# v cast to bfloat16 inside its own transfer, issued by GpSimd, in an attention and token-mixing kernel

## The chip, the cores and the metric

The kernel runs on one core of a Trainium2 chip. A core has a matrix engine (PE in the profile; its weight loads are listed apart as PEld), a vector engine (DVE), a scalar engine (ACT), GpSimd (POOL) and a sync engine (SP), which here issues transfers and computes nothing. Each engine works through its own instructions in order and waits on semaphores of the others. Transfers run on 16 DMA engines, whoever issues them. The metric is the device time of one execution in microseconds; the kernel before took 190.26, 190.16 and 189.40 us in three runs, a median of 190.16 us.

## The reference

Two stages in sequence, for 8 batches, 12 heads, 448 positions and a head size of 64, all in float32 outside:

```
scores = q @ k^T / sqrt(64) - log(448)          # per batch and head
attn   = 1 / (1 + exp(-scores))                 # a sigmoid, no softmax
x      = attn @ v, heads laid side by side      # (8, 448, 768)
wq, wk = x @ w_q, x @ w_k                       # (8, 448, 64)
W_tok  = wq @ wk^T / sqrt(64)
out    = relu(W_tok @ x) @ w_out                # (8, 448, 768)
```

## The kernel before

**Tiling.** The 96 heads are taken four at a time: 24 quads (8 batches of 3 quads). For one quad, q, k and v are 448 KB of float32 each; a tile has 128 partitions with 2 x 448 elements in each, because 64 partitions hold 7 positions apiece of a head, and two pairs of heads lie in the two halves. A quad has seven blocks of positions. For a block `scores` (L303) makes four 64-row matmuls into a pair of PSUM banks, ACT turns them into a bfloat16 tile with one sigmoid (L308), and `values` (L321) multiplies v into it, summing over the seven blocks. After the seventh the sum is copied to the x tile (L330, L328). The token-mixing stage of a batch (L361 and L344 transposes, L387 and L400 projections, L431, L471 and L483 mixing, L516, L556 and L600 the last product) is woven between the attention work of later quads.

**How the inputs come in.** SP issues the loads in float32 into six buffers `lds`, used in rotation by everything that is loaded: q, k and v of each quad and the weights. `pump_loads` issues the next entry of the list `ORDER` when the entry six places earlier has been cast (`ring[-6] not in cast`). From there the data are cast to bfloat16. GpSimd (engine "g") does most casts, at L198 (v, and q and k of some quads), L188 (q and k of the other quads, in another layout, followed for most of them by three pairs of copies at L157, L160 and L163) and L737 and L741 (weights); entries of `ORDER` with a dot are cast by DVE. q and k have two bfloat16 buffers each, or two for both where they share one; v has four (`p_v16`).

**What sets the order.** `PLAN` is a string written by hand: one letter for each piece of PE work, and the program is issued letter by letter. S is a `scores` block, P or p a `values` block. GpSimd's order is that of `ORDER`: `pump` walks it and casts an entry when `ready` says that it is loaded, that the one before of its kind is cast, and that the bfloat16 buffer it takes is used up (for v: quad n-4's last `values` has been issued). It stops at the first entry that is not ready. So v of a quad stands in GpSimd's queue among the casts of q and k of later quads, which wait for the transposes of earlier ones (L259, L252, L228 on DVE; L212 and L220 on PE).

**Lines the change touches.** `load1` (L165) issues a load on SP: L175 for v. `cast1` (L183) casts it: L198. `values` reads the v tile as weights at L322. `ORDER` stands at L686, `pump_loads` at L708. The first quad's q and k are cast in pieces by a loop of their own at L777 to L783, before the general order starts.

Of the kernel before, what the change touches and what calls it, by code (L numbers as in the profile page):

```python
# [10 lines left out]
BF16 = mybir.dt.bfloat16  # L11
# [6 lines left out]
def kernel(  # L18
# [12 lines left out]
    nc = tc.nc  # L31
    B, H, S, HD = q.shape
# [3 lines left out]
    P = 128  # L36
    NI, NP = 7, 64
# [4 lines left out]
    HALF = (slice(0, 64), slice(64, 128))  # L42
# [5 lines left out]
    def pool(name, bufs, **kw):  # L48
        return ctx.enter_context(tc.tile_pool(name=name, bufs=bufs, **kw))

    singles = pool("singles", 1)
    p_c16 = pool("c16", 2)
    p_v16 = pool("v16", 4)
# [17 lines left out]
    def bank2():  # L71
        n = free2.pop(0)
        return n, pairs[n], pairs16[n]
# [9 lines left out]
    def release(fb):  # L83
        if isinstance(fb, int):
            free2.append(fb)
        elif (fb[0], 1 - fb[1]) in halves:
            halves.remove((fb[0], 1 - fb[1]))
            free2.append(fb[0])
        else:
            halves.append(fb)  # L90
# [16 lines left out]
    def ld_next():  # L107
        nld[0] += 1
        return lds[(nld[0] - 1) % 6]

    def ld_next2():
        return ld_next().rearrange("p (b x) -> p b x", b=2)
# [3 lines left out]
    quads = [(u, j) for u in range(NU) for j in range(NJ)]  # L116
# [3 lines left out]
    def xt(u, j):  # L120
        return xts[u % 2 * NJ + j]
# [21 lines left out]
    ld = {}  # L143
# [4 lines left out]
    def arrange(n, eng):  # L148

        arranged.add(n)  # L150
        if KIND[n] in "er":
            return
        w = pq[n].rearrange("p e t i d y -> p e (t i d y)").bitcast(U32)
        z = p_one.tile([P, 2 * NI * 32], U32, tag="swap", name="swap")
        for g in range(2):
            lo, hi = slice(64 * g, 64 * g + 32), slice(64 * g + 32, 64 * g + 64)
            eng.tensor_copy(out=z[lo], in_=w[hi, 0])  # L157
        for g in range(2):
            lo, hi = slice(64 * g, 64 * g + 32), slice(64 * g + 32, 64 * g + 64)
            eng.tensor_copy(out=w[hi, 0], in_=w[lo, 1])  # L160
        for g in range(2):
            lo = slice(64 * g, 64 * g + 32)
            eng.tensor_copy(out=w[lo, 1], in_=z[lo])  # L163

    def load1(n, nm, eng):  # L165
        u, j = quads[n]
        if KIND[n] in "cer" and nm != "v":
            t = ld_next()
            eng.dma_start(
                out=t, in_=SRC[nm][u, 4 * j : 4 * j + 4].rearrange("h (p r) d -> (h p) (r d)", r=2 * NI),  # L170
            )
            ld[nm, n] = t
            return
        t = ld_next2()
        eng.dma_start(  # L175
            out=t,
            in_=SRC[nm][u, 4 * j : 4 * j + 4].rearrange(
                "(g h) (p i) d -> (h p) g (i d)", g=2, i=NI
            ),
        )  # L180
        ld[nm, n] = t

    def cast1(n, nm, e):  # L183
        if KIND[n] in "cer" and nm != "v":
            if n not in pq:
                pq[n] = p_c16.tile([P, 2, 2, NI, 32, 2], BF16, tag="qk16", name="qk16")
            f = pq[n]
            COPY[e](  # L188
                out=f[:, :, "qk".index(nm)].rearrange("p e i d y -> p e y i d"),
                in_=ld.pop((nm, n)).rearrange("p (y i e d) -> p e y i d", y=2, i=NI, e=2),  # L190
            )
            ld[nm + "16", n] = f
            if ("q16", n) in ld and ("k16", n) in ld:
                arrange(n, nc.gpsimd)
            return
        p = p_v16 if nm == "v" else p_c16
        t16 = p.tile([P, NI, 2, HD], BF16, tag=nm + "16", name=nm + "16")
        COPY[e](  # L198
            out=t16.rearrange("p i b d -> p b i d"),
            in_=ld.pop((nm, n)).rearrange("p b (i d) -> p b i d", i=NI),  # L200
        )
        ld[nm + "16", n] = t16
# [111 lines left out]
    def values(n, i, tail, eng):  # L314
        u, j = quads[n]
        if i == 0:
            pv[n] = bank2()
        fb, ps, _ = pv[n]
        for h in range(2):
            for g in range(2):  # L320
                nc.tensor.matmul(  # L321
                    ps[HALF[g], h, 0:S], ld["v16", n][HALF[h], i, g, :],  # L322
                    ats[n, i][HALF[h], g, :], start=(i == 0), stop=(i == NI - 1),
                )
        if i == NI - 1:
            if tail:
                for h in range(2):
                    COPY["vs"[h]](out=xt(u, j)[:, h, 0:S], in_=ps[:, h, 0:S])  # L328
            else:
                COPY[eng](out=xt(u, j)[:, :, 0:S], in_=ps[:, :, 0:S])  # L330
            release(fb)
# [309 lines left out]
    def load_weights():  # L641
        w32["qk"] = ld_next()[:, 0:D]
        for x, w in enumerate((moe_w_q, moe_w_k)):
            nc.sync.dma_start(
                out=w32["qk"].rearrange("p (c n) -> p c n", c=NC)[:, :, 64 * x : 64 * x + 64],
                in_=w.rearrange("(c p) n -> p c n", p=P)
            )

    def load_wout(c):
        w32[c] = ld_next()[:, 0:D]  # L650
        nc.sync.dma_start(out=w32[c], in_=moe_w_out[c * P : (c + 1) * P, :])
# [9 lines left out]
    def cols(r):  # L661
        return slice(r.start * HD, r.stop * HD)
# [8 lines left out]
        out=ident, in_=ident, compare_op=ALU.not_equal, fill=1.0, base=0,  # L671
# [10 lines left out]
    for n in range(7):  # L682
# [1 line left out]


    ORDER = (  # L686
# [5 lines left out]
    )  # L692
    BY = {"s": [], "v": []}
    for x in ORDER.split():
# [9 lines left out]
    used, loaded, cast = set(), set(), set()  # L704

    ring = [("q", 0), ("k", 0)]

    def pump_loads():  # L708
        while len(loaded) < len(ORDER):
            nm, n = ORDER[len(loaded)]  # L710
            if len(ring) >= 6 and ring[-6] not in cast:
                break
            ring.append((nm, n))
            if nm == "w":
                load_wout(n - 1) if n else load_weights()
            else:
                load1(n, nm, nc.sync)
            loaded.add((nm, n))
            issued[nm, n] = done["S"]
# [13 lines left out]
    def cast_now(nm, n, e):  # L733
        if nm != "w":
            cast1(n, nm, e)
        elif n:
            COPY[e](out=wout16[:, n - 1, :], in_=w32[n - 1])  # L737
        else:
            for h in range(2):
                for g in range(2):  # L740
                    COPY[e](  # L741
                        out=wqk16[HALF[g], h::2],
                        in_=w32["qk"].rearrange("p (c n) -> p c n", c=NC)[HALF[h], g::2],
                    )
        cast.add((nm, n))
        pump_loads()

    pumped = [0]
# [20 lines left out]
    def cast_by_others():  # L769
        while cast_one("s") or cast_one("v"):  # L770
            pass

    pump_loads()
    q016 = p_c16.tile([P, NI, 2, HD], BF16, tag="q16", name="q16")
    k016 = p_c16.tile([P, NI, 2, HD], BF16, tag="k16", name="k16")
    K1, K2, K3, K4 = slice(0, 1), slice(1, 3), slice(3, 5), slice(5, 7)
    for t16, t32, r, e in (  # L777
        (q016, q0, IA, "v"), (q016, q0, IB, "s"), (k016, k0, K1, "g"), (k016, k0, K2, "g"), (k016, k0, K4, "g"),
    ):
        COPY[e](  # L780
            out=t16[:, r].rearrange("p i b d -> p b i d"),
            in_=t32[:, :, cols(r)].rearrange("p b (i d) -> p b i d", d=HD),
        )  # L783
    qk[0] = p_qk.tile([P, 2, 2, NI, NP], BF16, tag="qk", name="qk")

    def tr_part(nm, t16, r, e):
# [13 lines left out]
        out=k016[:, K3].rearrange("p i b d -> p b i d"), in_=k0[:, :, cols(K3)].rearrange("p b (i d) -> p b i d", d=HD),  # L800
    )
    cast |= {("q", 0), ("k", 0)}
    pump_loads()
    used |= {("q", 0), ("k", 0)}
    pump()
# [6 lines left out]
    for t in PLAN:  # L812
# [10 lines left out]
        elif kind == "P":  # L823
            n, i = divmod(c, NI)
            values(n, i, tail, "s" if t == "p" else "v")
            if i == NI - 1:
                used.add(("v", n))
# [14 lines left out]
        elif t == "z":  # L842
            n = quads_r.pop(0)
# [17 lines left out]
        elif kind == "M":  # L861
            u, x = divmod(c, NC // 2)
# [44 lines left out]
```

## Time and profile before

| what | value |
|---|---|
| median of three runs | 190.16 us (189.40 to 190.26) |
| profiled execution: span, first to last instruction | 187.3 us |
| median less that span (the profile lists no other time for its own execution) | 2.9 us |
| PE busy | 176.1 us, 94% |
| ACT busy | 163.6 us, 87% |
| DVE busy | 141.1 us, 75% |
| POOL busy | 106.5 us, 57% |
| POOL casts of v, L198 | 22 x 931 ns = 20.4 us |
| DVE casts of v, L198 | 2, 585 and 1011 ns |
| loads of v, 448 KB each | 24 on SP's queue, median 6.4 us from issue to landing |
| DMA traffic | 48.97 MB, 261 GB/s on average |
| granted TensorE clock | 0.997 |

Times in the profile are microseconds from the first instruction unless marked ns. A row such as `L198 POOL CAST v<-ld` names the line of the kernel, the engine, the operation and the tiles written and read. In a timeline the first number is the start and the second the length of what may be several merged instructions (x4 is four of them); the bracket at its end is the idle time of the engine before it and what ended that. Busy time of PE is modelled and counts pipelined matmuls, so 94% is not PE at its peak. The median time to landing is counted from the issue on SP.

### The profile page before, as it was taken

The page shows a single profiled execution, that of the slowest core. Times are in us where ns is not written, and L with a number is a line of the kernel's source. Part 1 is how long each engine was busy: PE and PEld are TensorE (multiplying, and loading weights), DVE is VectorE, ACT ScalarE, POOL GpSimd, SP SyncE. Part 2 cuts the span into 40 slices and gives each one's busy share as a digit, 9 for nine tenths or more (in the row PEclk, how much of TensorE's full clock was granted, in tenths as well). Part 3 has the DMA queues.
Part 4 walks back from the last instruction along what each step waited for, and adds up shares of the span by engine and source line. Part 5 has one row for each costly group of instructions (what it writes and reads, how often), then busy time and mean ns, then how long its engine had stood idle before and what let it go on. Part 6 is the DMA issues. An engine that isn't in the chain of part 4 may idle for free.

```text
span 187.3 us, 8513 instructions
## 1 busy us (share of the span) xinstructions
PE 176.1 (94%) x3648; PEld 115.9 (62%) x3648; DVE 141.1 (75%) x223; ACT 163.6 (87%) x210; POOL 106.5 (57%) x145
## 2 busy tenths in 40 slices
PE   7898899989999999999999999998999999999990
PEld 7443556544555454565555776766998889786660
DVE  3354697577868999999898999977778665697810
ACT  4799999999999989999999999996999989984230
POOL 1437798972968989899999892486033900000000
PEclk9999999999999999999999999999999999999998
DMA  5999999964699989989998995984998634513395
GB/s 173 340 390 383 309 354 366 390 244 142 198 361 402 405 293 298 353 265 314 310 315 267 296 410 192 281 271 143 275 307 276 149 101 113 128 50 76 97 241 177
DMA packets 26469, 48.97 MB, mean 261 GB/s; under 512 B 4096, under 2 KB 20352, under 8 KB 26432
## 3 DMA queue, kind: packets, MB, share of 16 engines
q1 hardware_dynamic: 26272, 48.24, 79.3%
q8 instruction: 28, 0.46, 1.0%
q10 hardware_dynamic: 160, 0.20, 0.4%
q14 instruction: 9, 0.07, 0.1%
HBM read 35.78 MB, written 11.01 MB: 250 GB/s over the span
## 4 chain that ended last, share of the span: by engine, by line
PE 69%; DVE 15%; ACT 9%; issue 4%; ACTq 0%; DVEq 0%
PE banks L303 15%; PE banks L516 13%; PE banks L321 12%; PE banks L600 10%; ACT at L308 9%; DVE qk L228 4%; DVE xt L330 3%; PE banks L556 3%; PE banks L387 3%; DVE mx L459 2%; PE banks L431 2%; PE banks L361 2%; PE banks L344 2%; PE banks L677 2%; PE banks L471 1%
## 5 line engine op out<-in xcount | busy, mean ns | idle before, releaser
L308 ACT ACTIVATE at<-banks 128x896 bf16<-128x896 f32 x168 | 141.7, 927 | 5.4 <-PE banks L303 4.2
L303 PE MATMUL banks<-qk 64*64 64x448 bf16 x672 | 63.6, 359 | 4.2 <-ACT at L308 1.1
L321 PE MATMUL banks<-at,v 64*64 64x448 bf16 x672 | 46.6, 350 | 0.2
L303 PEld LDWEIGHTS <-qk 64*64 64x64 bf16 x672 | 26.0, 105 | 27.2 <-issue 16.2
L516 PE MATMUL banks<-wout,mx 64*64 64x384 bf16 x672 | 35.1, 323 | 0.0
L188 POOL CAST qk<-ld 128x896 bf16<-128x896 f32 x24 | 28.5, 1206 | 9.9 <-DVE qk L259 6.7
L198 POOL CAST v<-ld 128x896 bf16<-128x896 f32 x22 | 20.4, 931 | 15.2 <-PE banks L303 10.0
L321 PEld LDWEIGHTS <-v 64*64 64x64 bf16 x672 | 23.1, 106 | 7.8 <-issue 1.7
L516 PEld LDWEIGHTS <-mx 64*64 64x64 bf16 x672 | 24.2, 107 | 3.5
L459 DVE TENSOR_SCALAR mx<-banks 128x1024 bf16<-128x1024 f32 (+2 forms) x21 | 21.1, 1010 | 5.6 <-PE banks L483 3.3
L600 PE MATMUL banks<-wout,mx 128*128 128x384 bf16 (+1 forms) x138 | 24.7, 320 | 0.0
L330 DVE CAST xt<-banks 128x896 bf16<-128x896 f32 x20 | 21.6, 1083 | 3.7 <-PE banks L321 2.1
L600 PEld LDWEIGHTS <-mx 128*128 128x128 bf16 x138 | 11.9, 98 | 10.4 <-issue 4.5
L259 DVE STREAM_TRANSPOSE qk<-qk 128x448 f32<-128x448 f32 x24 | 15.0, 630 | 0.0
L396 POOL COPY wq<-wqk 64x448 bf16<-64x448 bf16 x6 | 3.7, 620 | 18.4 <-DVE wqk L395 18.1
L163 POOL COPY qk<-swap 32x448 uint32<-32x448 uint32 x20 | 11.8, 592 | 1.2
L525 DVE COPY o<-banks 128x768 f32<-128x768 f32 x9 | 8.6, 955 | 4.8 <-PE banks L516 4.8
L157 POOL COPY swap<-qk 32x448 uint32<-32x448 uint32 x20 | 11.1, 554 | 1.8 <-DVE qk L188 0.7
L160 POOL COPY qk<-qk 32x448 uint32<-32x448 uint32 x20 | 11.1, 554 | 1.2
L228 DVE STREAM_TRANSPOSE qk<-qk 32x448 f32<-32x448 f32 x16 | 10.2, 636 | 0.4
L374 DVE COPY xn<-banks 128x1024 bf16<-128x1024 bf16 (+1 forms) x13 | 8.2, 628 | 3.0 <-PE banks L361 1.9
L387 PE MATMUL banks<-xt,wqk 64*64 64x448 bf16 x144 | 9.9, 350 | 0.0
(94 smaller groups left out, 217.2 us busy)
## 6 DMA issues: line engine op xcount, KB each, us to landing
ld<-in_q_dram SPq DMA_DIRECT2D x24, 448.0 KB, 6.2
ld<-in_v_dram SPq DMA_DIRECT2D x24, 448.0 KB, 6.4
ld<-in_k_dram SPq DMA_DIRECT2D x23, 448.0 KB, 6.1
out_dram<-o SPq DMA_DIRECT2D x42, 192.0 KB, 4.1
ld<-in_moe_w_out_dram SPq DMA_DIRECT2D x6, 384.0 KB, 5.0
out_dram<-ld SPq DMA_DIRECT2D x11, 192.0 KB, 2.8
wout<-wout SPq DMA_DIRECT2D x12, 96.0 KB, 5.8
qk<-mv SPq DMA_DIRECT2D x8, 56.0 KB, 3.3
```

The costliest lines, as they stand in the source:

```text
L188: COPY[e](out=f[:, :, "qk".index(nm)].rearrange("p e i d y -> p e y i d"), in_=ld.pop((nm, n)).rearrange("p (y i e d) -> p e y i d", y=2, ...
L198: COPY[e](out=t16.rearrange("p i b d -> p b i d"), in_=ld.pop((nm, n)).rearrange("p b (i d) -> p b i d", i=NI),)
L228: nc.vector.transpose(out=qk[n][other : other + 32, h].rearrange("p t i n -> p (t i n)").bitcast(F32), in_=w[own : own + 32, 1 - h],)
L259: nc.vector.transpose(out=qk[n][:, t].rearrange("p t i n -> p (t i n)").bitcast(F32), in_=w)
L303: nc.tensor.matmul(sc[HALF[h], g, 0:S], qk[n][HALF[g], h, 1, i, :], qk[n][HALF[g], h, 0].rearrange("p i n -> p (i n)"), start=True, stop=True,
L308: nc.scalar.activation(at, sc[:, :, 0:S], ACTF.Sigmoid, bias=attn_bias, scale=attn_scale)
L321: nc.tensor.matmul(ps[HALF[g], h, 0:S], ld["v16", n][HALF[h], i, g, :], ats[n, i][HALF[h], g, :], start=(i == 0), stop=(i == NI - 1),)
L330: COPY[eng](out=xt(u, j)[:, :, 0:S], in_=ps[:, :, 0:S])
L387: nc.tensor.matmul(ps[HALF[x], y, 0:S], wqk16[HALF[y], c, 64 * x : 64 * x + 64], xt(u, c // 2)[HALF[y], c % 2, 0:S], start=(c == 0), stop= ...
L459: nc.vector.tensor_scalar(dst, ps, moe_scale, 0.0, ALU.mult, ALU.max)
L516: nc.tensor.matmul(ps[HALF[x], y, 0:NB], mx[HALF[y], u, b, 64 * (i - 3 * y) : 64 * (i - 3 * y) + 64], wout16[HALF[y], slot(y, b), x * NB : ...
L600: nc.tensor.matmul(ps, mxs[w][:, 2 * S * c + m * P : 2 * S * c + (m + 1) * P], wout16[:, c, w0:w1], start=(c == 0), stop=(c == NC - 1),)
```

## The change

v no longer passes through a float32 buffer. `load1` returns at once for v; where v was cast, `cast1` now issues on GpSimd's queue a transfer that reads float32 from memory and writes bfloat16 straight into one of the four v buffers. `values` waits for that transfer where it waited for the cast. The tile's layout changes from (block, pair, 64) to (pair, block, 64), so that a partition's row in memory is a run of the tile; the matmul's weight slice is again 64 neighbouring elements. `pump_loads` counts v as loaded without giving it a place in the ring, so the six float32 buffers hold q, k and weights only. The first v is issued right after the second piece of k's first cast, and v of quads 16 and 21, cast by DVE before, now stands in GpSimd's queue as the others do.

```diff
     def load1(n, nm, eng):
+        if nm == "v":
+            return
         u, j = quads[n]
...
-        p = p_v16 if nm == "v" else p_c16
-        t16 = p.tile([P, NI, 2, HD], BF16, tag=nm + "16", name=nm + "16")
+        if nm == "v":
+            u, j = quads[n]
+            v16 = p_v16.tile([P, 2, NI, HD], BF16, tag="v16", name="v16")
+            nc.gpsimd.dma_start(
+                out=v16.rearrange("p b i d -> p b (i d)"),
+                in_=v[u, 4 * j : 4 * j + 4].rearrange("(g h) (p i) d -> (h p) g (i d)", g=2, i=NI),
+            )
+            ld["v16", n] = v16
+            return
+        t16 = p_c16.tile([P, NI, 2, HD], BF16, tag=nm + "16", name=nm + "16")
...
-                    ps[HALF[g], h, 0:S], ld["v16", n][HALF[h], i, g, :],
+                    ps[HALF[g], h, 0:S], ld["v16", n][HALF[h], g, i, :],
...
     ORDER = (
-        "q1 .k1 v0 q2 .k2 v1 k3 q3 q4 k4 v2 w0 v3 k5 k6 q5 "
+        "v0 q1 .k1 q2 .k2 v1 k3 q3 q4 k4 v2 w0 v3 k5 k6 q5 "
...
-        "v13 q15 k15 .q16 v14 .q17 k16 v15 .v16 k17 q18 k18 k19 v17 .k20 q19 "
-        "k21 .q20 .k22 v18 q21 .k23 q22 v19 v20 .v21 v22 v23 q23 "
+        "v13 q15 k15 .q16 v14 .q17 k16 v15 v16 k17 q18 k18 k19 v17 .k20 q19 "
+        "k21 .q20 .k22 v18 q21 .k23 q22 v19 v20 v21 v22 v23 q23 "
...
-            if len(ring) >= 6 and ring[-6] not in cast:
-                break
-            ring.append((nm, n))
+            if nm != "v":
+                if len(ring) >= 6 and ring[-6] not in cast:
+                    break
+                ring.append((nm, n))
...
             in_=t32[:, :, cols(r)].rearrange("p b (i d) -> p b i d", d=HD),
         )
+        if r is K2:
+            cast_now("v", 0, "g")
+            pumped[0] += 1
```

## The prediction

> **What bounds the kernel now.** I read the page's busy rows and slices first, then the groups, then GpSimd's timeline beside PE's at the places where v is cast and used.
>
> ```profile
> ACT  4799999999999989999999999996999989984230
> POOL 1437798972968989899999892486033900000000
> DMA  5999999964699989989998995984998634513395
> ...
> L308 ACT ACTIVATE at<-banks 128x896 bf16<-128x896 f32 x168 | 141.7, 927 | 5.4 <-PE banks L303 4.2
> L198 POOL CAST v<-ld 128x896 bf16<-128x896 f32 x22 | 20.4, 931 | 15.2 <-PE banks L303 10.0
> ```
>
> The slices show ACT full from slice 3 to 33. The sums over a stretch say the same: from 6.5 to 167 us ACT is busy 155.0 of 160.5 us. Its sigmoids are fed by PE just in time, in PE's order, so a pause of PE costs ACT nearly its whole length and cannot be made up before 167 us. GpSimd's 57% hides a stretch from about 54 to 113 us where it is nearly full, but no long wait of PE names it: its v casts cost the end nothing now.
>
> What matters is how long before its use a v cast starts. GpSimd's timeline, then PE's:
>
> ```profile
> 45.56 0.56 POOL L409 COPY wq<-wqk 64x448 bf16<-64x448 bf16 x1 [4.43 <-DVE wqk L405]
> 46.18 0.93 POOL L198 CAST q<-ld 128x896 bf16<-128x896 f32 x1
> ...
> 49.48 0.93 POOL L198 CAST v<-ld 128x896 bf16<-128x896 f32 x1
> ...
> 119.84 1.20 POOL L188 CAST qk<-ld 128x896 bf16<-128x896 f32 x1 [5.95 <-DVE qk L259]
> 120.94 0.94 POOL L198 CAST v<-ld 128x896 bf16<-128x896 f32 x1
> ```
>
> ```profile
> 51.66 0.38 PE L303 MATMUL banks<-qk 64*64 64x448 bf16 x4
> 51.87 0.55 PE L321 MATMUL banks<-at,v 64*64 64x448 bf16 x8
> ...
> 122.61 1.12 PE L321 MATMUL banks<-at,v 64*64 64x448 bf16 x20
> ```
>
> Quad 7's cast starts 2.39 us before its first use (49.48 to 51.87), quad 18's 2.05 us (120.94 to 122.99; the first eight of the x20, 0.38 us, are quad 17's). Both times GpSimd had waited for DVE just before, so it cannot come there earlier. The load was the early part: the issues and their landings read
>
> ```profile
> ld<-in_v_dram SPq DMA_DIRECT2D x24, 448.0 KB, 6.4
> ...
> DMA to landing us min/median/max: 3.1/6.6/8.3
> ```
>
> where the second line is for all loads of L175, and its 3.1 is v of quad 7, issued at 40.28 us behind a short queue.
>
> **The change, part by part.** *Casts removed.* 22 x 0.93 = 20.4 us leave POOL and 0.58 + 1.01 = 1.6 us DVE. POOL's are beside ACT's work. DVE's two fall where ACT is full, so I take 0 for them, with a gain of 1.6 us as the bound.
>
> *Issues moved.* 24 issues leave SP (0.37 us each undisturbed, no bound there) and come to POOL, at the casts' places: `ready` asks the same of v as before, and walking `pump` through PLAN gives the same order on POOL except that v16 joins it behind v15, and v20 to v22 come up behind v19, ahead of batch 5's wq copy (129.31 us, not read before the mixing near 142 us). So the transfer starts where the cast started, and its whole length now lies between that place and the use. The wait for the buffer (quad n-4's last `values`) is the cast's old one; behind it stand q and k casts and the copies for which L259 on DVE waits. At v22 and v23 that buffer is free at 125.6 and 137.8 us, first uses are at 161 and 163 us, and DVE needs q23 at 150.8 us: nothing.
>
> *What POOL pays for an issue* is not in the trace. Lowest is an undisturbed SP issue, 0.37 us; highest an SP issue held up, 7.08 us for three at L651, 2.4 each. I take 1.0, nearest to the cast that it replaces on the same engine (0.93), since POOL has to work for it; POOL's pace then stays as it is.
>
> *From issue to landing*: 3.1 us alone (quad 7's row) to 6.4 us (the median, behind SP's backlog). v now has a queue of its own beside SP's loads. One other load of 448 KB that takes turns with it adds its own time, 459 kB at the 370 GB/s of 7 to 20 us = 1.24 us: 3.1 + 1.24 = 4.3 us. So from POOL's start to data, D = 5.3 us, between 0.37 + 3.1 = 3.5 and 2.4 + 6.4 = 8.8.
>
> The Trainium skill (DMA: Bandwidth & Descriptors, Anatomy of one DMA — SWDGE (gpsimd) path) fits such a DMA as a whole at 2.0 us plus bytes over 436 GB/s, here 3.05 us as an estimate, and the one lone load in the trace agrees (3.1 us, though issued by SP); with that for D the sum below would be 1.4 us.
>
> *Stalls.* The PE pause at a quad is D, less the time from POOL's start to first use (margin), less the slack between the next scores' end and their sigmoid's start (0.06 to 0.37 us, from PE's and ACT's timelines):
> - v1: q2's cast ends at 12.86, POOL then idles; use at 16.89: 5.3 - 4.03 - 0.06 = 1.2. v2: 20.50 to 23.56: 5.3 - 3.06 - 0.23 = 2.0. POOL is held there by landings and itself, not by PE, so v2's includes v1's: 2.0. v3 (margin 4.57) is then covered.
> - v7: 5.3 - 2.39 - 0.37 = 2.5.
> - v9, v11, v12 (65.12 to 67.97, 74.53 to 77.17, 82.22 to 85.01): 2.3, 2.5, 2.4. POOL is its own pace there, so a pause gives the next v more time; I count the largest, 2.5. v8 and v14 (margins 4.94, 5.22) follow from it for nothing.
> - v18: 5.3 - 2.05 - 0.12 = 3.1. v19 has 7.1 us, the others 7 or more.
>
> Together 2.0 + 2.5 + 2.5 + 3.1 = 10.1 us.
>
> *The start.* v0 is issued at about 5.3 us, after K2's cast, instead of 3.26 on SP; with D it is there at 10.6, and its first matmul is at 12.19: no stall. But its transfer now takes turns with q1 and k1, which were ahead of it; k1's copy (11.30, L276) releases scores with no slack. Between 0 and one load's 1.24 us; I take the middle, 0.6.
>
> *The ring.* With v out of it, q, k and weights are loaded up to two places earlier. POOL's waits for q and k landings (1.15 us before 56.77) may go; ACT does not wait for them. 0, and up to 1.2 us less at v9.
>
> Sum: 187.3 + 10.1 + 0.6 = 198.0 us of span. The median stands 2.9 us above the profiled span: 200.9, forecast **201 us**. With D = 4 the four stalls are 5.0 us, 195.8; with D = 6.8 they are 16.1, 207.
>
> **The rivals.** *Covered after all (faster or same).* If issue and landing together take 3.1 us, the stalls are 0.3 (v7), 0.3 (v11) and 0.9 (v18), and DVE's 1.6 us and fewer POOL waits offset them: 190.16 + 1.5 - 1.6 = 190 us, and at D below 3.1 it is faster, down to 188.6. It decides at the margins of v7 and v18. For it: the 3.1 row, and DMA share is only 0.62 from 37 to 52 us. Against: that row already is 3.1 without GpSimd's issue, and from 70 to 113 us the share is 0.95 or more.
>
> The skill's fit above, taken as the whole of D, ends in this rival too.
>
> *POOL becomes the bound (much slower).* At 2.4 us for an issue, POOL gains 1.5 us with each of ten v between 54 and 113 us, 15 us against some 4 us of idle time; q and k for L259 then come late too (now from 0.4 us ahead, quad 21, to about 4), and D is 6.7 to 8.8: stalls of 15.7 to 24, so 207 to 215 us. For it: POOL is at 9 tenths there, and its copies stretch when DVE casts from SBUF (L163's pair 1.63 us at 96.53 beside DVE's casts at 97.07, else 1.16). Against: DVE has only ten or so such casts, and none at v2, v7 or v18. A slow conversion in the DMA engines, which no row shows, would look alike.
>
> *The ring wins.* q and k arrive earlier and POOL runs ahead. Against: POOL at v7 and v18 is held by DVE, not by loads; it trims v9 by 1.2 us at most and is inside the forecast's range.
>
> **How the numbers follow.** Forecast 0.68 (D from 4 to 6.8: 195.5 to 207), POOL-bound or a longer D 0.20 (207 to 215), covered 0.12 (188.6 to 195). A measurement of this kernel can tell 0.5%, 0.95 us, from no change; of the 0.12, 0.06 is below 189.2, 0.03 within, 0.03 slower. So faster 0.06, same 0.03, slower 0.91. The range leaves out the covered case and the far end of the long one: 194 to 213.
>
> **What would show it.** PE's L321 should wait for a DMA into v, some 2 to 3 us at quads 2, 7, 18 and one of 9 to 12, with ACT's idle time before L308 up from 5.4 us to about 15; GpSimd's issue row should read about 1.0 us, the landing 4.3 us, POOL's order unchanged. Wrong if the landing is near 3 us and PE waits for nothing, or if POOL's issues are so long that L259 waits for L163.

## The result, and the profile after

The changed kernel takes 213.51 us (211.12 to 215.00 in four runs) against 190.21 us of the kernel before, run beside it (189.40 to 190.63): a ratio of 1.121, 95% interval 1.113 to 1.129. The forecast was 201 us within 194 to 213; the sign is right, the size is about double (+23.3 us against +10.8). The profiled execution of the changed kernel is the longest of its four, 215.0 us with a span of 213.1 us; it lies over 1.5% above the shortest and is left out of the ratio.

The page's slices of PE and of its granted clock before:

```profile
PE   7898899989999999999999999998999999999990
PEclk9999999999999999999999999999999999999998
```

After, with ACT and POOL, whose slices before stand in the prediction, and PE's busy row:

```profile
PE 181.6 (85%) x3648; PEld 116.6 (55%) x3648; DVE 138.2 (65%) x221; ACT 164.8 (77%) x210; POOL 102.7 (48%) x147
...
PE   7876969989619999659999999943999999999990
ACT  3877869999807999919999999950889998994420
POOL 2447944925958329780999885296203610001000
PEclk9999699999958999979999999995899999999999
```

Where ACT was full from slice 3 to 33 there are now holes, the deepest in slices 11, 17 and 27, counted from 0, and PE has holes in the same places. PE's clock, full up to the last slice before, now falls in slices 4, 11, 17 and 27 too (and 12 and 28 behind them). The groups for ACT's sigmoids, PE's `values` and GpSimd's issues (busy time and mean; then idle time before them and what ended most of it), and the issue row (KB written, median us from issue to landing), after the row of `values` before:

```profile
L321 PE MATMUL banks<-at,v 64*64 64x448 bf16 x672 | 46.6, 350 | 0.2
```

```profile
L318 ACT ACTIVATE at<-banks 128x896 bf16<-128x896 f32 x168 | 142.4, 924 | 29.6 <-PE banks L313 27.7
L331 PE MATMUL banks<-at,v 64*64 64x448 bf16 x672 | 50.3, 373 | 21.3 <-DMA v<-in_v_dram 20.1
...
L201 POOL DMA_DIRECT2D v<-in_v_dram x24 | 17.3, 721 | 13.7 <-PE banks L331 8.9
...
v<-in_v_dram POOLq DMA_DIRECT2D x24, 224.0 KB, 7.2
```

The sigmoids are the same work (142.4 us against 141.7), but ACT's idle time before them went from 5.4 to 29.6 us. That is +24.2 us, nearly all of the 25.8 us by which the span grew (213.1 against 187.3). PE's `values` waited 20.1 us for transfers into v. PE's own account of the 25.8 us has two parts: idle time 31.5 us (213.1 - 181.6) against 11.2 (187.3 - 176.1), 20.3 us more, and busy time 181.6 us against 176.1, 5.5 us more for the same matmuls. GpSimd spends 0.72 us on an issue, less than the 0.93 us of the cast that it replaces, and is busy 102.7 us instead of 106.5. The landing takes 7.2 us in the median.

The chain that ended last (start, length, what it was) has the transfers that cost most, each followed by the first matmuls that use them. All are of the `values` line:

```profile
20.17 8.36 DMA v<-in_v_dram
28.57 0.57 PE banks L331 x8
...
54.23 8.71 DMA v<-in_v_dram
62.98 0.96 PE banks L331 x8
...
85.70 7.11 DMA v<-in_v_dram
92.86 1.95 PE banks L331 x20
...
138.43 8.91 DMA v<-in_v_dram
147.39 1.33 PE banks L331 x10
```

These are quads 2, 7, 11 and 18, the four places that the prediction had named. What it had wrong is the second column.

### The profile page after: what moved, and what is told of

The parts are those of the page before. It is cut to its first block, busy times and chain, and to the rows that moved or that the text cites. A ratio compares the mean times of both kernels' runs of the same rounds, so it can differ in the third digit from the quotient of the medians.

```text
span 213.1 us, 8468 instructions
## 1 busy us (share of the span) xinstructions
PE 181.6 (85%) x3648; PEld 116.6 (55%) x3648; DVE 138.2 (65%) x221; ACT 164.8 (77%) x210; POOL 102.7 (48%) x147
## 2 busy tenths in 40 slices
DMA packets 26469, 43.47 MB, mean 204 GB/s; under 512 B 4096, under 2 KB 20352, under 8 KB 26432
## 3 DMA queue, kind: packets, MB, share of 16 engines
q1 hardware_dynamic: 19744, 37.23, 55.6%
q0 software_dynamic: 6528, 5.51, 17.7%
## 4 chain that ended last, share of the span: by engine, by line
PE 49%; DMA 23%; DVE 8%; POOL 6%; issue 5%; ACT 4%; SPq 1%; ACTq 0%; POOLq 0%; DVEq 0%
DMA v<-in_v_dram 16%; PE banks L331 10%; PE banks L313 9%; PE banks L526 9%; PE banks L610 8%; DMA ld<-in_k_dram 7%; ACT at L318 4%; PE banks L397 3%; PE banks L566 3%; POOL qk L190 2%; DVE xt L340 2%; DVE qk L238 2%; DVE mx L469 2%; PE banks L371 1%; PE banks L493 1%
## 5 line engine op out<-in xcount | busy, mean ns | idle before, releaser
L318 ACT ACTIVATE at<-banks 128x896 bf16<-128x896 f32 x168 | 142.4, 924 | 29.6 <-PE banks L313 27.7
L331 PE MATMUL banks<-at,v 64*64 64x448 bf16 x672 | 50.3, 373 | 21.3 <-DMA v<-in_v_dram 20.1
L313 PE MATMUL banks<-qk 64*64 64x448 bf16 x672 | 64.7, 370 | 2.7 <-ACT at L318 0.6
L469 DVE TENSOR_SCALAR mx<-banks 128x1024 bf16<-128x1024 f32 (+2 forms) x21 | 21.1, 1010 | 13.3 <-PE banks L493 10.4
L201 POOL DMA_DIRECT2D v<-in_v_dram x24 | 17.3, 721 | 13.7 <-PE banks L331 8.9
L397 PE MATMUL banks<-xt,wqk 64*64 64x448 bf16 x144 | 10.5, 367 | 0.0
L404 DVE COPY wpart<-banks 128x448 f32<-128x448 f32 x6 | 3.7, 620 | 9.9 <-PE banks L397 9.9
```

What stands on the lines that cost most here:

```text
L201: nc.gpsimd.dma_start(out=v16.rearrange("p b i d -> p b (i d)"), in_=v[u, 4 * j : 4 * j + 4].rearrange("(g h) (p i) d -> (h p) g (i d)", g ...
L313: nc.tensor.matmul(sc[HALF[h], g, 0:S], qk[n][HALF[g], h, 1, i, :], qk[n][HALF[g], h, 0].rearrange("p i n -> p (i n)"), start=True, stop=True,
L318: nc.scalar.activation(at, sc[:, :, 0:S], ACTF.Sigmoid, bias=attn_bias, scale=attn_scale)
L331: nc.tensor.matmul(ps[HALF[g], h, 0:S], ld["v16", n][HALF[h], g, i, :], ats[n, i][HALF[h], g, :], start=(i == 0), stop=(i == NI - 1),)
L397: nc.tensor.matmul(ps[HALF[x], y, 0:S], wqk16[HALF[y], c, 64 * x : 64 * x + 64], xt(u, c // 2)[HALF[y], c % 2, 0:S], start=(c == 0), stop= ...
L469: nc.vector.tensor_scalar(dst, ps, moe_scale, 0.0, ALU.mult, ALU.max)
```

## The experiments

"Margin" is the prediction's word: the time from the place of the cast in GpSimd's queue to the first use of that v by PE.

**Twelve of the 24 taken back.** The kernel before, with twelve v, mostly those with the larger margins, moved into GpSimd's transfers; the twelve others (quads 0 to 4, 7 to 9, 11, 12, 14 and 18) are loaded by SP and cast as before.

```diff
+    VD = {5, 6, 10, 13, 15, 16, 17, 19, 20, 21, 22, 23}
     def load1(n, nm, eng):
+        if nm == "v" and n in VD:
+            return
...
     def cast1(n, nm, e):
...
+        if nm == "v" and n in VD:
...
```

> The quads whose cast stood less than 6 us before its use in the kernel before (0, 1, 2, 3, 4, 7, 8, 9, 11, 12, 14, 18) are loaded by SP in float32 and cast by GpSimd as before; the other twelve keep the casting transfer at its late place. Theory A: those twelve have 7 us or more, so PE waits for none of them by more than 1 us: 189 to 192 us. Theory B: about half of the 23 us remains, 200 to 203 us.

Measured: 189.76 us (ten runs) against 189.15, ratio 1.005 (1.0011 to 1.009). Half of the transfers cost next to nothing; the 23 us hang on the other half. Not on all moved work, then, but on the places. PE's one wait for a transferred v in it (total, times, longest):

```profile
PE banks L339 <- DMA v<-in_v_dram: 1.3, 1, 1.3
```

**One alone.** The reverse: the kernel before, with quad 18 alone as in the change (`VD = {18}`, the rest as in the diff above).

> The kernel before with one v alone, quad 18's, moved to a casting transfer at the place of its cast. Theory A: a wait of PE for that transfer of its length (7 to 9 us beside SP's loads) less the 2.2 us of margin: 195 to 197 us. If the transfer's length is my forecast's 5.3 us instead: 193.2. Theory B, with 23 us spread over 24 transfers: 191 us.

Measured: 194.04 to 198.01 us in four runs, median 196.74, against 189.15. The profiled execution took 195.76 us, 6.6 us more. Two waits of it, and the landing of that transfer:

```profile
PE banks L339 <- DMA v<-in_v_dram: 4.5, 1, 4.5
ACT at L326 <- PE banks L321: 9.5, 11, 5.3
```

```profile
DMA to landing us min/median/max: 6.6/6.6/6.6
```

With one moved v GpSimd has no more to do than before, so it cannot be GpSimd's work that costs. A margin of 2.05 us against a landing of 6.6 us costs PE 4.5 us, as the subtraction says (6.6 - 2.05 = 4.55). ACT loses 5.3 us, and the time grows by more than that.

**One alone, with PE kept busy.** The kernel above, with 24 matmuls of zeros ahead of quad 18's `values` (work added, its result overwritten), so that PE does not rest while v is on its way.

```diff
+        if n == 18 and i == 0:
+            for _ in range(24):
+                nc.tensor.matmul(ps[:, 0], zeros[:, 0:P], zeros, start=True, stop=True)
```

> The run with quad 18 alone, plus 24 matmuls of zeros just ahead of quad 18's first value matmul, some 5 us of work that PE does while it would wait, so that PE doesn't rest. If the fall of PE's clock after the pause (0.982 in that run against 0.997) is part of the 7.6 us: 194.5 to 196 us, with the clock back at 0.99 or above. If only the wait counts: 196.7 us, within 0.8.

Measured: 193.89 us (193.00 to 194.19) against 188.63, ratio 1.026 (1.0212 to 1.0307), just under the range expected if the clock counts. The slices of the granted clock, first of quad 18 alone and then with PE kept busy:

```profile
PEclk9999999999999999999999999958999999999999
```

```profile
PEclk9999999999999999999999999999999999999998
```

Quad 18 alone in stretches of 1 us (start and end; length; busy time and instructions of PE, its weight loads, DVE, ACT, POOL; then the granted clock, DMA share and GB/s):

```profile
123.00:124.00 1.00, 0.37 (x8) 0.00 (x0) 1.00 (x2) 1.00 (x2) 0.88 (x3) 1.00 0.91 135
...
125.00:126.00 1.00, 0.00 (x0) 0.00 (x0) 1.00 (x2) 0.00 (x0) 0.88 (x3) 0.86 1.05 340
126.00:127.00 1.00, 0.00 (x0) 0.00 (x0) 0.02 (x1) 0.00 (x0) 0.88 (x3) 0.50 1.02 284
...
131.00:132.00 1.00, 1.00 (x20) 0.42 (x14) 0.00 (x0) 0.47 (x1) 0.59 (x1) 0.50 0.03 13
132.00:133.00 1.00, 1.00 (x20) 0.53 (x16) 0.00 (x0) 0.59 (x2) 0.00 (x0) 0.72 0.00 0
```

PE stops at 123.4. The clock is at half from about 125.7 and comes back at about 132.6, some 4.7 us after the matmuls went on at 127.84. With PE kept busy it never falls. What that costs is read from PE's timelines, from quad 18's first `values` to the first large group of the last product, first of quad 18 alone, then with PE kept busy, and the last product's first group in the kernel before:

```profile
127.84 1.33 PE L339 MATMUL banks<-at,v 64*64 64x448 bf16 x12 [4.46 <-DMA v<-in_v_dram]
...
133.19 1.14 PE L534 MATMUL banks<-wout,mx 64*64 64x384 bf16 x24
```

```profile
128.05 0.76 PE L342 MATMUL banks<-at,v 64*64 64x448 bf16 x12
...
131.10 1.15 PE L537 MATMUL banks<-wout,mx 64*64 64x384 bf16 x24
```

```profile
126.02 1.15 PE L516 MATMUL banks<-wout,mx 64*64 64x384 bf16 x24
```

The same matmuls take 5.35 us in the one and 3.05 us in the other; in the kernel before, from 122.99 to 126.02, 3.03 us. So one pause of 4.5 us costs another 2.3 us behind it. The timelines show this, not the whole times: those all but meet (194.04 to 198.01 us, and 193.00 to 194.19 with PE kept busy), and the zeros themselves held PE 1.5 us beyond the landing (126.54 to 128.05).

**Eight buffers.** The change with eight v buffers instead of four, the issues where they were: does the wait for a free buffer hold them?

```diff
-    p_v16 = pool("v16", 4)
+    p_v16 = pool("v16", 8)
...
-        back = 4 if nm == "v" else 2
+        back = 8 if nm == "v" else 2
```

> The changed kernel with eight v buffers and nothing else, the part that the two runs with earlier places shared. If the places did it and the buffers nothing: 210 to 215 us, PE's waits for v about 21 us as in the changed kernel. If a wait for a free buffer was the cause: below 200 us.

Measured: 209.38 and 218.81 us in two runs, with PE waiting 16.7 us for v. Most of the loss is still there, so the buffers are not the main of it.

**Issued earlier.** The change with eight buffers and v earlier in `ORDER`, in two versions. Counted in the lists, the one called "six earlier" moves v7 by six entries, most others by four or five, the last three by two or three and v0 not at all; the one called "three earlier" moves most by two or three, v21 by one, and v0, v22 and v23 not. Both move less than the expectations say.

```diff
-        "v0 q1 .k1 q2 .k2 v1 k3 q3 q4 k4 v2 w0 v3 k5 k6 q5 "
+        "v0 v1 q1 .k1 q2 v2 .k2 v3 k3 q3 q4 k4 v4 w0 v5 k5 "
...
-        "k21 .q20 .k22 v18 q21 .k23 q22 v19 v20 v21 v22 v23 q23 "
+        "q19 k21 v19 .q20 v20 .k22 v21 v22 q21 v23 .k23 q22 q23 "
```

> Every v but the first stands six entries earlier in the order list, and v has eight bfloat16 buffers in place of four, so that an early v does not wait for one. Nothing else is changed against the changed kernel. Theory A (the loss is the late start: a v transfer of 7 to 9 us from GpSimd's queue to its landing, begun where the cast began): PE's waits for v shrink from 21 us to about the first quad's 1 us, and the time is 188.5 to 192 us. Theory B (a transfer issued by GpSimd costs wherever it stands, by its issue, by its conversion or by what it takes from the loads of q and k): it stays above 200 us.

> As the run with six entries, but three entries earlier. Theory A: the margins grow by some 3 to 7 us, enough for quads 11 and 18, not for quad 7, whose v then stands about 4.8 us before its use (stall about 3.5 us) nor quite for quads 0 and 2 (together about 2.5 us): 194 to 199 us. Theory B: no better than six entries, above 200 us.

Measured: six earlier 191.42 us (ratio 1.0134, 1.0071 to 1.0197), three earlier 191.48 us (1.0139, 1.0056 to 1.0221), both against 189.15. PE's waits for v and the landings, six and then three earlier:

```profile
PE banks L331 <- DMA v<-in_v_dram: 0.9, 1, 0.9
```

```profile
PE banks L331 <- DMA v<-in_v_dram: 0.8, 2, 0.5
```

```profile
DMA to landing us min/median/max: 3.6/8.1/10.8
```

```profile
DMA to landing us min/median/max: 4.1/7.7/10.2
```

Some 21 of the 23 us are gone, though the same 24 issues still stand on GpSimd, convert as they did, and take longer to land than in the change (8.1 and 7.7 us in the median against 7.2). So all but some 2 us of what the change costs is the place of the issue. Three earlier did better than expected: quad 7's v came down in 4.46 us, at 52.23, 0.36 us ahead of its use; had it taken its 8.7 us of the change, PE would have waited 3.9 us.

**The first two as before.** What PE still waits for v in these versions is at v0 and v1, for which there is no earlier place. So: v0 and v1 loaded by SP and cast, the others by transfer, placed as in "three earlier"; and a mixed one, with v2 four entries earlier, v3 to v18 as in "six earlier" and v19 to v23 as in "three earlier". Both with eight buffers; the lines show the mixed one.

```diff
+    VD = {2, 3, 4, 5, 6, 7, 8, 9, 10, 11, 12, 13, 14, 15, 16, 17, 18, 19, 20, 21, 22, 23}
...
+        "q1 .k1 v0 q2 .k2 v1 v2 v3 k3 q3 q4 k4 v4 w0 v5 k5 "
```

> A version meant to be good: quads 0 and 1 by SP and a cast as in the kernel before, all others by the casting transfer three entries earlier with eight buffers. It takes away the start's 1 to 1.5 us that the run with three entries still lost to quads 0 and 1. 188 to 189.5 us beside 189.2 for the kernel before: the same within 0.5%, or faster by at most that. If the casting transfers cost something beyond their lateness: 190.5 us or more.

> As the version with quads 0 and 1 left with SP, but six entries earlier up to quad 18, so that no v lands within a few us of its use, and three entries for 19 to 23, where six had made four transfers meet the moves of quad 20. If what is left of that version's 1.2% is that v's now and then lands just late (its quads 7 and 8 had 0.4 and 0.1 us in the profile of three entries): 188 to 189.3 us beside 188.9 of the kernel before. If the casting transfers cost something besides: 190.5 us or more.

Measured: placed as in "three earlier" 191.35 us against 188.63 (ratio 1.0124, 1.0041 to 1.0206), a miss; the mixed one 190.05 us (twelve runs) against 189.13, ratio 1.0042 (1.0007 to 1.0076), also above what was expected. In the mixed one ACT's idle time is that of the kernel before, and its waits list no transfer into v:

```profile
L326 ACT ACTIVATE at<-banks 128x896 bf16<-128x896 f32 x168 | 141.9, 925 | 4.9 <-PE banks L321 3.7
```

So the change can be brought to 0.4% above the kernel before, and nothing here brought it below.

**DVE's two casts alone.** The kernel before with only v16 and v21 moved (`VD = {16, 21}`), the two that DVE cast: is its 1.6 us worth anything?

> The kernel before with only the two v that DVE cast, quads 16 and 21, moved to the casting transfer on GpSimd, 10 us and more ahead of their use. The 1.6 us of DVE work are the one saving that could reach ACT's path: if they do, by ACT's 1.4 us of idle time near 131 us, 187.5 to 188.4 us beside 188.9; if DVE's casts were covered: 188.9 within 0.5 us.

Measured: 189.54 us against 189.13 (twelve and 23 runs), ratio 1.000 (0.9966 to 1.0035). Nothing, as the prediction took it.

**Why the landing takes so long.** In the trace each packet is recorded. For the changed kernel, from the end of GpSimd's issue to the first packet of that v, to its last, and to the landing, in us, with the number of SP's transfers that were issued and not landed at the end of the issue (worked out from the trace):

```
quad   first   last   landed   SP's under way
 0      3.37   6.71    7.03      5
 1      3.26   6.86    7.27      7
 2      3.21   5.79    7.65      6
 7      3.41   7.23    8.00      3
11      2.99   5.90    6.39      5
18      2.27   7.49    8.20      5
12      0.70   2.44    2.91      1
22      0.70   2.72    3.03      0
23      0.71   2.70    3.17      2
```

Where little of SP's was before it, v needed 0.7 us to its first packet and 1.7 to 2.0 us from there to its last; where SP's loads of 448 KB were queued, it waited 2.3 to 3.4 us for the first and was then interleaved with more of them. v14 and v19 had seven of SP's under way and still began after 0.7 to 0.8 us; six of each seven were smaller ones, so the mere count is not the cause. The bytes fit. What SP had issued and not yet begun to move at the end of the issue was 2.0, 1.7, 1.5, 1.2, 1.0 and 0.8 MB at quads 0, 1, 2, 7, 11 and 18, nothing at 12 and 22, 0.1 MB at 23, and 0.3 and 0.2 at 14 and 19. Over the traces of all versions, leaving out each v with another v's packets before it, the first packet came after 0.70 to 0.72 us in all 14 cases with less than 0.1 MB left, after 2.0 us in the median with 0.5 to 1.0 MB (0.9 to 3.1, 27 cases), and after 3.0 to 3.8 us in all ten with more than 1.3 MB. Two tests of the backlog: the rule that lets SP load when the entry six earlier is cast, set to three,

```diff
-                if len(ring) >= 6 and ring[-6] not in cast:
+                if len(ring) >= 3 and ring[-3] not in cast:
```

> The changed kernel with three float32 buffers in the ring's rule in place of six, so that SP runs at most three loads ahead. Theory Q (a v transfer stands behind what SP has queued: first packet 3.3 us after the issue where loads are in flight, 0.7 us where none are): the first packet comes after 1 to 2 us and the median landing falls from 7.2 to 4.5 to 5.5 us, and PE's waits for v from 21 to about 10 us. Theory P (the conversion or GpSimd's queue is slow in itself): landing stays at 7 us. The total is no test, since q and k come later: 200 to 220 us.

and then also three float32 buffers in place of six (`range(6)` and `% 6` to 3).

> The changed kernel with three float32 buffers in fact, not only in the rule, so that SP can have at most three loads between issue and cast. Theory Q (v stands behind and beside what SP has queued): in quads 0, 1, 2, 7, 11 and 18 the time from the issue's end to the first packet falls from about 3.3 us to 1 to 2, and the landing of quad 7's v from 8.0 us after the issue's end to 4 to 6. Theory P (the path is slow): unchanged. The total is again no test, since q and k come later: 200 to 235 us.

The first was ill made: SP still had its six buffers and as many transfers under way (six or seven at v0 to v2), so it says nothing of the backlog; it took 224.76 us in two runs. With three buffers, two or three transfers of SP's were under way at v0 to v3 and v7, and the first packets came after 1.64 (v0), 1.73, 1.03, 1.95 (v3) and, at v7, 1.66 us, half of what they were or less but for v3 (2.53). The landings of all 24:

```profile
DMA to landing us min/median/max: 3.6/5.7/8.6
```

The median fell from 7.2 to 5.7 us, v7's landing from 8.0 to 5.2 us after the issue's end. So at those quads SP's backlog is what v waits behind. At v11 and v18 the expected fall came in part: the first packet after 1.89 us instead of 2.99, but the landing after 7.46 instead of 6.39 at v11; the first packet no sooner (2.30), the landing after 6.54 instead of 8.20 at v18. There four and five transfers were still under way, among them stores. The wait for the first packet is only one part: with quad 18 alone, 0.3 MB of SP's were left and the first packet came after 0.99 us, yet v's packets were spread over 4.5 us and landed 5.82 us after the issue's end. The kernel as a whole got slower, 224.9 us (ratio 1.19), as q and k now came late too. PE's waits for v and GpSimd's for q in it:

```profile
PE banks L331 <- DMA v<-in_v_dram: 27.0, 7, 6.8
...
POOL qk L190 <- DMA ld<-in_q_dram: 21.6, 8, 7.9
```

## Why the prediction was right and wrong

**Right.** The mechanism: GpSimd's queue puts the issue where the cast was, and the transfer is then exposed at quads 2, 7, one of 9 to 12 (11), and 18. GpSimd kept its order, and its own pace does not bound the kernel; the rival in which it becomes the bound did not happen, though the time of 207 to 215 us that it shared with "a longer D" did, by the second. DVE's two casts were worth 0. An issue took 0.72 us, inside the bounds of 0.37 to 2.4 us and under the 1.0 us taken.

**The step that failed is "From issue to landing".** It took 3.1 us for a lone load and added one other load in turn, 1.24 us: 4.3 us. At the four stalls it took 7.11 to 8.91 us from the start of the issue (forecast D: 5.3 us). The other steps of these stalls then hold, but for quad 2. The prediction's formula, D less margin less slack, with the measured D:

| quad | forecast stall | measured D | formula with it | PE idle, measured |
|---|---|---|---|---|
| 2 (with 1) | 2.0 | 8.36 | 8.36 - 3.06 - 0.23 = 5.1 | 1.5 + 1.8 = 3.3 |
| 7 | 2.5 | 8.71 | 8.71 - 2.39 - 0.37 = 6.0 | 6.2 |
| 11 | 2.5 | 7.11 | 7.11 - 2.64 - 0.14 = 4.3 | 3.9 |
| 18 | 3.1 | 8.91 | 8.91 - 2.05 - 0.12 = 6.7 | 6.7 |
| sum | 10.1 | | 22.1 | 20.1 |

Quad 2's is below the formula; ahead of it v0 had held PE for another 1.0 us, and PE's clock was at half from 21.35 to 24.77 us, so its first use came later. The rival in which all is covered needed a D near 3.1 us; only the transfers with nothing in their way came near that, and they stood at places with room.

The row for a long landing stood in the profile of before: the median of 6.4 us for loads behind SP's backlog. The prediction kept it for the end of the range and took the lone one, on the ground that v has a queue of its own. That was the error. At quads 2, 7 and 18 SP's loads are already queued in front when GpSimd issues, several of them and not one, and a queue of its own did not take v past them: of v7's 3.4 us to its first packet, 2.7 us are waiting, by the difference to the 0.7 us of an undisturbed one. The nearer row was that with the same backlog: 6.4 us, against the 6.39 to 8.20 us from the issue's end to the landing at these four quads. Nor did turns with one load describe the rest of the way: the packets of v7 were spread over 3.8 us, twice the 1.7 to 2.0 us of v12, v22 and v23.

The fit of the Trainium skill (DMA: Bandwidth & Descriptors, Anatomy of one DMA — SWDGE (gpsimd) path), 2.0 us plus bytes over 436 GB/s, gives 3.05 us as an estimate. It agrees with the quads where nothing was in the way (2.91 us at v12, 3.03 at v22, after the issue's end), and is less than half of the 7.0 to 8.2 us at v0 to v2, v7 and v18. The same page of the Trainium skill (Queues, rings and completion order) says that each DMA engine goes round the queues that have work, a packet of some 9 to 17 descriptors at a time. Turns are seen here once v has begun (993 kB of SP's packets started between v7's first packet and its last), but how long one is is not shown; before v7's first packet 1,038 kB of SP's went, more than two loads.

**"v0: no stall"** was wrong too, for the same reason: issued at 5.30, it was there at 13.15 instead of 10.6, and PE waited 0.97 us, ACT 1.07. On the other side, the 0.6 us for k1's delayed load did not come: the scores that its copy releases start at 11.85 us, 11.98 before. And the reading that the quads not named had 7 us or more left out quad 4, whose margin is 5.45 us (28.48 to 33.93); it cost nothing, as its v landed at 35.10 and was used at 38.69.

**A term that was missing** is the half clock after a pause. It adds to ACT's idle time what PE's does not show: 20.1 + 1.0 = 21.1 us of pauses of PE, 24.2 us more of ACT's. PE's busy time is 5.5 us longer; that this is the half clock is argued from the slices, and the experiment with PE kept busy shows it for one pause: 2.3 us for one of 4.5 us. The prediction's sum has no such term. Of the 15.1 us by which the span passed the forecast (213.1 against 198.0), the longer stalls are 10.0 (20.1 - 10.1) and the longer busy time 5.5.

In the changed kernel the clock is at half in four stretches: 58.90 to 65.73 us at quad 7 (PE idle from 56.79 to 62.98), 93.03 to 96.45 at quad 11 (idle 88.91 to 92.86), 144.23 to 151.06 at quad 18 (idle 140.66 to 147.39), and 21.35 to 24.77 us, behind quad 1's pause of only 1.49 us (18.09 to 19.59). The lines for the last, as for quad 18 alone above:

```profile
20.00:21.00 1.00, 1.00 (x17) 0.24 (x9) 0.00 (x0) 0.60 (x1) 0.88 (x2) 1.00 1.11 383
21.00:22.00 1.00, 0.81 (x11) 0.73 (x8) 0.00 (x0) 1.00 (x2) 0.61 (x2) 0.68 1.01 371
22.00:23.00 1.00, 1.00 (x14) 0.80 (x16) 0.00 (x0) 0.93 (x2) 0.90 (x3) 0.50 1.07 382
```

So the length of a pause does not decide alone. In all 13 traces here the clock's changes lie a whole number of steps of 3.41 us apart, so the time can be cut into windows of that length, counted from the first change (worked out from the traces). Of the 698 windows that ran at full clock, it fell after each of the 30 in which PE was idle for 49% or more, and after none of the others (at most 48% idle). Of the 30 at half clock, it came back after each of the 18 with at most 20% idle and after none of the 12 with 28% or more. PE's idle share is the profile's, whose busy time of PE is modelled.

The Trainium skill (TensorE: Matmul & The Clock Gate, What's actually happening) says that PE falls to half rate after an idle window of about 3.4 us and needs about as long a busy one to come back. The trace agrees with the two rates (1.00 and 0.50) and with the length of the window, but here a window about half idle was enough.

**What stays open.** The versions with earlier issues are 0.4 to 1.4% above the kernel before, with ACT's idle time before its sigmoids (4.9 to 5.6 us) near that of before (5.4). In three of the four traces ("three earlier" and both with the first two as before) the last sigmoid ends at 163.9 us as in the kernel before, and the 0.8 to 1.3 us that the span is longer lie behind it, where no v is awaited. That v now and then lands just too late would fit the spread of their runs (190.28 to 193.40 us for "three earlier" with the first two as before), and so would v7's 0.36 us to spare in "three earlier", but no trace here shows such a late one. In "six earlier" ACT lost 1.75 us at 137 us, close behind four v issued between 121 and 124 us; that these delayed quad 20's own data was not tested.

## What to carry to other kernels

A load on one queue and a cast on another are two places in time, and a transfer that casts is one: put at the cast's place, it exposes the whole transfer, so it has to be issued where the load was, here with a margin of up to 9 us where the 0.93 us cast was content with 2. Price a transfer by rows that had the same backlog beside them, not by a lone one (a queue of its own is not a way past what others have queued), and a pause of PE at more than its length, for the half clock that can follow: it did after every pause of 3.9 us or more here, and after some of 1.5 to 2.1 us.

## What the runs showed of the hardware that was not expected

- GpSimd pays 0.71 us (median 714 ns; 832 ns for the first) to issue a 128 x 2 x 448 casting transfer, less than the 0.93 us to cast the same data.
- The conversion costs little DMA time. By the queues' rows (packets, MB, time as a share of 16 engines' span) the casting queue's packets took 17.7% of 16 engines' 213.1 us for 6528, 92 ns each; SP's, 55.6% for 19744, 96 ns each, but of mixed sizes. Like with like: the 6144 casting packets that read 1,792 bytes and write 896 took 97 ns in the mean, SP's 4096 packets of 1,792 bytes 85 ns (84 in the kernel before).

```profile
q1 hardware_dynamic: 19744, 37.23, 55.6%
q0 software_dynamic: 6528, 5.51, 17.7%
```

- A transfer on GpSimd's queue waited for its first packet 0.70 us undisturbed and 3.0 to 3.8 us with more than 1.3 MB of SP's loads issued and not begun; three buffers, which kept that backlog short, brought 1.0 to 2.0 us at the first quads and at quad 7.
- Of two v issued one behind the other, the second began where the first ended: v10, issued 0.7 us after v9, had its first packet 2.76 us after its issue, at v9's last (74.14 us), with two stores of SP's under way.
- The granted clock of PE was judged in windows of 3.41 us: it fell to half after each with 49% or more of it idle and came back after each with at most 20% idle. The fall came 2.1 to 4.1 us after PE stopped for the three long pauses, the return 2.7 to 3.7 us after it went on.
- Of the kernel, not the chip: the rule six or three entries back did not set how much SP had under way (five to seven transfers at v0 to v2 with six, six or seven with three); the number of buffers did.
